# Block attention and expert layers on one core: the last pair's softmax sums on TensorE, weight copies and squares moved between engines, slot 0's second layer moved ahead of slot 1

## The chip, the cores and the metric

The kernel runs on one core of a Trainium2 chip. The metric is the time of one execution on the device, in microseconds (us); lower is better. Of the kernel before, three runs were timed and one more execution was profiled.

## What is computed

```python
scores = scale * np.matmul(q, k.transpose(0, 1, 3, 2))      # q, k, v: 8 x 8 x 576 x 64
scores = np.where(block_i >= block_j, scores, -1e9)         # blocks of 64 positions
attn = exp(scores - max);  attn = attn / sum(attn)
x = (attn @ v), heads side by side                          # 4608 tokens x 512
logits = normalised x @ normalised expert_emb.T / tau       # 8 experts
expert = argmax(logits);  gate = softmax(logits)[expert]
out[token] = gate * (relu(x @ w1[expert]) @ w2[expert])     # w1 512 x 1024, w2 1024 x 512
```

Attention is block-causal. Each token then goes through one of eight experts, the one with the largest logit.

## The kernel before

**Attention.** The 64 heads are worked on in 32 pairs (n = 0 to 31), a pair being two heads of one batch. `scores` makes the scores transposed, keys on the partitions, in five key tiles t of 128 keys (the last has 64); ScalarE takes the exponentials into `pT` (L378, L385). `add` (L359) has GpSimd add the tiles t = 1 to 4 into `pS`, so that `pS` and tile 0 hold, per query, what has to be summed over 128 partitions. One pair later `values` multiplies the probabilities with V into the PSUM tile `psb` (L398), ScalarE copies the result to `oe` (L404), and TensorE sums with matmuls whose stationary side is the constant `ones` with 32 columns: four column groups g, one for each 128 queries (L413, L416). Beside them come the router's logits from `enT` and `oe`. `su` (L418) takes the sums out of PSUM. `finish` turns `su` and `oe` by TensorE (L428, L430), divides on VectorE (L435 to L445, which read `psb`), stores rows and, in the last batch, takes squares on ScalarE (`squares`, L464). The pool `ps_b` has one buffer, so the values of a pair wait until `finish` of the pair before has read it.

**The order.** In the loop over pairs a string of letters (`PLANS`) writes the order out by hand: s is a step of `scores`, v of `values` of the pair before, f of `finish` of that pair, r of the router. Each engine and the queues of SyncE (SP) and GpSimd (POOL) execute in program order.

**Between attention and experts.** Weights arrive as f32 in `raw0` (w1) and `raw1` (w2), in four chunks of 128 x 1024 (c = 0 to 3). Each chunk is split into a high part `ring_h` (a rounding copy, `split_hi`, L731) and a low part `ring_l` (raw minus high, `split_lo`, L736, on VectorE); a product is three matmuls, high·high, low·high and high·low (`mm3`, L931). A ring tile has two halves. Two "early" slots a and b of 128 tokens (`ex0`, `ex1`) hold tokens of expert 0 from the first seven batches; their rows are gathered by GpSimd (L584). While the last pair is finished and the last batch is routed, TensorE works on a and b: `xt` turns their rows (L918), ScalarE and VectorE split these into high and low (L921, L922), `l1` and `l2` are the two layers. `chain()` is the routing of the last batch, step by step between the pieces of `l1` and `l2`: `finish` of pair 31, `route`, `counts`, `slot_tokens`, and the gathers of the first slots (`fetch`, L909). `second(c)` makes the high and low part of chunk c of expert 0's w2; `again` the same for the other ring; `next_weights` those of expert 1.

**Slots.** Then slots g of 128 tokens each follow: `layer1` (24 matmuls), `xt` of the next slot, the turn of h, and the second layer of the slot before. For slot 1 the turn is done by TensorE (`mixed`, `ht`); for later slots by VectorE (L977).

The steps that the change touches, as they stand before:

```python
for c in range(NPC):                       # L1061
    split_hi(0, c, 0, eng=nc.gpsimd if c == 2 else nc.scalar)
    split_lo(0, c, 0)
    if c < 2:
        drain(pv, 4)                       # values of pair 31
    if c == 1:
        drain(pv)                          # sums of pair 31
        for u, g in enumerate(ea):
            xt(g, pts[u], hx if u else None)
```

Of the kernel before, what the change touches and what calls it, by code (L numbers as in the profile page):

```python
# [8 lines left out]
F32 = mybir.dt.float32  # L9
# [25 lines left out]
def kernel(  # L35
# [12 lines left out]
    nc = tc.nc  # L48
# [312 lines left out]
    def scores(n, pTs):  # L361

        i = n % NBUF
        for hh, (pT, ps) in enumerate(pTs):

            def mm(o, t, c0, c1):
                ts = slice(t * P, (t + 1) * P)
                nc.tensor.matmul(o, ka[i][:, hh, ts], qb[i][:, hh, c0:c1], start=True, stop=False)  # L368
                nc.tensor.matmul(o, kx[i][0:KX, hh, ts], qx[i][0:KX, hh, c0:c1], start=False, stop=True)  # L369

            for t, c0, c1 in ((0, 0, S // 2), (0, S // 2, S), (1, P, S), (2, 2 * P, S)):
                if n == 0 and hh and c0 == 0:
# [12 lines left out]
            nc.scalar.activation(pT[:, off[3]:NPT], st[:, 0:256], AF.Exp, scale=scale)  # L385
            add(ps, 3, pT)
            add(ps, 4, pT)
            yield

    def values(n, pTs):  # L390

        a = vo[n % NV]
        ob = ps_b.tile([P, 1024], F32, name="psb")
        for t in range(NJ):
# [10 lines left out]
        yield  # L405
        for w in range(3):
            for g in range(NG):
                if w == 2:
                    a, m = enT[:, n % NP], o[:, g * P:(g + 1) * P]
                else:  # L410
                    pT, ps = pTs[w]
                    a, m = ones[:, w], ps[:, (g - 1) * P:g * P] if g else pT[:, 0:P]
                nc.tensor.matmul(ob[32 * g:32 * g + 32, 0:P], a, m, start=(w == 0), stop=(w == 2))  # L413
        for g, (a, m) in enumerate(((enT[:, n % NP], o[:, S - 64:S]),) + tuple(
                (ones[:, w % 2], pTs[w % 2][1][:, S - P - 64:S - P]) for w in range(3))):
            nc.tensor.matmul(ob[32 * g:32 * g + 32, P:LW], a, m, start=True, stop=True)  # L416
        yield
        nc.scalar.copy(su[n % 2][:, 0:LW], ob[:, 0:LW])  # L418
        yield

    def finish(n, xrow, rin, lgh, ssp):
# [29 lines left out]
        if n >= NPAIR - NP:  # L451
            yield "squares"
            for j in range(NJ):
                squares(xrow[:, j, hp * P:(hp + 1) * P], ssp[:, j, hp:hp + 1])
            yield

    def store(b, xrow, c0, c1):
# [11 lines left out]
    def route(b, xrow, lgh, ssp):  # L469
# [532 lines left out]
    def chain():  # L1002
# [15 lines left out]
        tw = two()  # L1018
        yield next(tw)
        next(rg)  # L1020
        for _ in range(5):
# [28 lines left out]
    hx = [mx.tile([P, NF // 2, P], F32R, name=nm) for nm in ("hh1", "hl1")]  # L1050
    psum_t.close()
    ps_e = pool(psum_t, "ps_e", 1, space=PSUM)
    pts = [ps_e.tile([P, 512], F32, name=f"pe{u}") for u in range(2)]
    ea = []
    for u in range(EARLY):
# [3 lines left out]
        slots[g]["w", 0] = half_of(0, 0)  # L1059
        slots[g]["w", 1] = half_of(0, 1)  # L1060
    for c in range(NPC):  # L1061
        split_hi(0, c, 0, eng=nc.gpsimd if c == 2 else nc.scalar)
        split_lo(0, c, 0)
        if c < 2:
            drain(pv, 4)
        if c == 1:
            drain(pv)
            for u, g in enumerate(ea):
                xt(g, pts[u], hx if u else None)
    load_raw(0, 1)  # L1070
# [52 lines left out]
    def second(c):  # L1123
        split_hi(1, c, 1, to=0)
        split_lo(1, c, 1, to=0)
# [6 lines left out]
    second(0)  # L1132
    drain(last_f)
    drain(ch_sq[0])
# [25 lines left out]
    next_weights(0, 0, (0, 1, 2))  # L1160
    l2(b, range(6, 7))
    for f in range(0, DF, 512):
        l1(0, range(NC1), f)
    xt(1, pts[1])
    l2(b, range(7, 8))
    fetch(AHEAD)
# [21 lines left out]
    def mixed(g):  # L1188

        pts = turn_pe(g)  # L1190
        out = take("py")
        mm3(g - 1, 1, out, slots[g - 1]["hT"], DM, NF, 0, range(4))
# [6 lines left out]
    def back(g):  # L1199
# [8 lines left out]
        if g == 1:  # L1208
            next_weights(0, 1, range(NPC))
            next_high(1, 0, range(NPC))  # L1210
# [38 lines left out]
    TURNED, FLAGS_AT = (1,), 1  # L1249
    pt0 = turn_pe(0)  # L1250
    ht(0, (0, 4), pt0, ("turn",))
    ht(0, (0, 4), pt0, ("split",))
    next_weights(0, 0, (3,))
    flags(1)
# [54 lines left out]
```

## Time and profile before

| | us |
|---|---|
| median of three runs | 867.73 (865.12 to 867.75) |
| profiled execution, its own time | 863.76 |
| its span | 862.0 |
| TensorE busy in the span | 829.6 |

The profiled execution is one more run, 3.97 us under the median; its span is the time from its first instruction to its last, 1.76 us less than its time. Attention fills the span up to about 402 us, the two early slots and the routing of the last batch reach to about 441 us, and the slots fill the rest at 11.4 us each. In rows of the timeline, the two numbers ahead of the engine are start and length in us; what stands in brackets is how long the engine was idle before, and who released it.

### The profile page before, as it was taken

To read this page: it belongs to the slowest core of one execution; us is meant where nothing else is said; L and a number is where in the kernel's file an instruction comes from. 1 tells how busy PE (TensorE), PEld (TensorE's weight loads), DVE (VectorE), ACT (ScalarE), POOL (GpSimd) and SP (SyncE) were. 2 spreads that over 40 slices of the span, in tenths; PEclk is the share of its full clock that TensorE was granted. 3 is DMA by queue.
4 is the path that set the end of the run, shared out by engine and by line. 5 is a ranking of instruction groups with operands and counts; after the bars stand their busy time and mean duration, and the time that the engine had idled before them with its cause. 6 is when DMAs were issued, how large, how long until landed. Compare 5 with 4: busy or idle time off the path is not lost. (4 is left out here: it accounts for less than half of the span.)

```text
span 862.0 us, 20599 instructions
## 1 busy us (share of the span) xinstructions
PE 829.6 (96%) x5609; PEld 663.7 (77%) x5609; DVE 658.3 (76%) x1539; ACT 479.0 (56%) x1027; POOL 447.6 (52%) x509
## 2 busy tenths in 40 slices
PE   5999999999999999997999999899999999999997
PEld 4777777777778887776778888688878888888885
DVE  7678878787878888764867887677887777778871
ACT  4566868676767868775565446454443233442232
POOL 5355575756567575676134647876472111572101
PEclk9999999999999999999999999999999999999999
DMA  7777777879677887837175525555252111012111
GB/s 153 168 164 162 181 190 180 210 172 219 153 195 161 211 176 158 205 111 245 55 253 176 172 96 174 190 177 185 86 180 90 52 51 51 28 49 72 39 35 48
DMA packets 155176, 122.31 MB, mean 142 GB/s; under 512 B 122217, under 2 KB 123513, under 8 KB 155020
## 3 DMA queue, kind: packets, MB, share of 16 engines
q1 hardware_dynamic: 147372, 100.14, 44.9%
q0 software_dynamic: 7648, 20.44, 7.4%
q8 instruction: 55, 0.90, 0.4%
q14 instruction: 101, 0.83, 0.3%
HBM read 72.71 MB, written 19.71 MB: 107 GB/s over the span
## 5 line engine op out<-in xcount | busy, mean ns | idle before, releaser
L977 DVE STREAM_TRANSPOSE pt<-h 32x256 f32<-32x256 f32 x528 | 240.7, 456 | 18.0
L339 DVE TENSOR_REDUCE nmx<-psm 128x1 f32<-128x320 f32 x315 | 135.5, 454 | 54.8 <-PE psm L338 50.0
L378 ACT ACTIVATE pT<-pss 128x448 f32<-128x448 f32 (+1 forms) x254 | 109.0, 450 | 83.2 <-PE pss L369 80.3
L991 POOL DMA_INDIRECT out_dram<-y,outi x36 | 35.8, 994 | 192.1 <-ACTq L885 138.1
L736 POOL TENSOR_TENSOR ring_l<-raw,ring_h 128x1024 f32 (+1 forms) x49 | 116.3, 2401 | 30.8 <-ACT ring_h L731 23.3
L359 POOL TENSOR_TENSOR pS<-pS,pT 128x320 f32<-128x320 f32 (+2 forms) x192 | 115.1, 600 | 27.2 <-ACT pT L378 10.4
L368 PE MATMUL pss<-qb,ka 128*128 128x448 f32 (+1 forms) x382 | 118.4, 322 | 0.0
L359 POOL TENSOR_TENSOR pS<-pT 128x448 f32<-128x448 f32 x64 | 73.1, 1142 | 78.5 <-ACT pT L378 77.9
L931 PE MATMUL py<-ring_h,hh 128*128 (+1 forms) x280 | 112.5, 402 | 1.1 <-ACT hh L983 0.6
L931 PE MATMUL py<-ring_h,hl 128*128 (+1 forms) x280 | 111.6, 398 | 0.8 <-DVE hl L985 0.8
L369 PE MATMUL pss<-qx,kx 70*128 70x448 f32 (+1 forms) x382 | 109.8, 310 | 1.3 <-DMA qx<-nmT 1.1
L931 PE MATMUL ph<-ring_l,xh 128*128 x280 | 109.2, 390 | 1.6 <-POOLq L897 0.9
L931 PE MATMUL ph<-ring_h,xh 128*128 x280 | 109.2, 390 | 0.7 <-ACT ring_h L731 0.7
L931 PE MATMUL py<-ring_l,hh 128*128 (+1 forms) x280 | 109.3, 390 | 0.0
L931 PE MATMUL ph<-ring_h,xl 128*128 x280 | 109.1, 390 | 0.0
L338 PE MATMUL psm<-kd,qd 128*128 128x320 f32 x315 | 106.6, 361 | 1.8 <-ACT kd L318 1.8
L398 PE MATMUL psb<-pT,vo 128*64 128x64 f32 (+4 forms) x768 | 99.2, 399 | 6.0 <-DVE lgh L445 5.5
L949 ACT ACTIVATE h<-ph 128x512 f32<-128x512 f32 x70 | 42.0, 600 | 90.0 <-DVE pt L977 78.9
L985 DVE TENSOR_TENSOR hl<-pt,hh 128x512 fp32r<-128x512 f32 x66 | 42.5, 687 | 61.2 <-ACT hh L983 59.0
L990 ACT ACTIVATE y<-py,xg 128x512 f32<-128x512 f32 x35 | 24.1, 688 | 110.6 <-PE py L931 110.6
L398 PEld LDWEIGHTS psb<-pT,vo 128*64 128x64 f32 x768 | 49.9, 138 | 44.3 <-issue 30.7
L731 ACT CAST ring_h<-raw 128x1024 f32 (+1 forms) x67 | 66.2, 1048 | 27.7 <-SPq L904 11.9
(260 smaller groups left out, 1622.5 us busy)
## 6 DMA issues: line engine op xcount, KB each, us to landing
raw<-in_moe_w_dram SPq DMA_DIRECT2D x64, 512.0 KB
ka<-kd SPq DMA_DIRECT2D x128, 144.0 KB
qn<-in_q_dram SPq DMA_DIRECT2D x64, 144.0 KB
kn<-in_k_dram SPq DMA_DIRECT2D x64, 144.0 KB
qx<-qb SPq DMA_DIRECT2D x32, 288.0 KB
vo<-in_v_dram SPq DMA_DIRECT2D x64, 128.0 KB
xbuf<-xrow SPq DMA_DIRECT2D x7, 1040.0 KB
qx<-nmT SPq DMA_DIRECT2D x64, 2.2 KB
```

The lines of the kernel that those rows point to most:

```text
L338: nc.tensor.matmul(mx[:, 0:e - a], qd[d][:, j, :, :], kd[d][:, a:e], start=True, stop=True)
L339: nc.vector.tensor_reduce(m[:, j + u:j + u + 1], mx[:, 0:e - a], axis=AX.X, op=ALU.max, negate=True)
L359: nc.gpsimd.tensor_tensor(o, pT[0:r, P:S] if t == 1 else o, pT[0:r, off[t]:off[t] + w], op=ALU.add)
L368: nc.tensor.matmul(o, ka[i][:, hh, ts], qb[i][:, hh, c0:c1], start=True, stop=False)
L369: nc.tensor.matmul(o, kx[i][0:KX, hh, ts], qx[i][0:KX, hh, c0:c1], start=False, stop=True)
L378: nc.scalar.activation(pT[:, o:o + c1 - c0], st[:, 0:c1 - c0], AF.Exp, scale=scale)
L398: nc.tensor.matmul(ob[hh * D:(hh + 1) * D, c0:c1], a[:, t, hh, :], pTs[hh][0][:, o:o + c1 - c0], start=(t == 0), stop=(c0 == 448 or t == N ...
L731: return (nc.scalar.copy if eng is nc.scalar else eng.tensor_copy)(piece(ring_h, to, c, half), raw[i][:, c * CW:(c + 1) * CW])
L736: return eng.tensor_tensor(piece(ring_l, to, c, half), raw[i][:, c * CW:(c + 1) * CW], piece(ring_h, to, c, half).bitcast(F32), op=ALU.sub ...
L931: m = nc.tensor.matmul(out, ac, w, start=(c == 0 and w is wh and a is sh), stop=(c == nk - 1 and a is sl_))
L977: nc.vector.transpose(pt[32 * j:32 * j + 32, :, 32 * i:32 * i + 32], h[32 * i:32 * i + 32, :, j, :])
L985: nc.vector.tensor_tensor(sets["hl"][u], pt[:, 4 * u:4 * u + 4], sets["hh"][u].bitcast(F32), op=ALU.subtract)
```

## The change

Five edits, all of them between the last pair of attention and slot 2:

1. Pair 31 does without GpSimd's adds. Its sums are made by TensorE from `pT` directly: for each head and key tile t, one matmul for each group g ≥ t (20 of 128 columns in place of 8) and 11 of 64 columns in place of 3. Its values go to the tile `pst`, its sums to `psb`.
2. The high parts of w1 of expert 0 are made in the order c = 2, 0, 1, 3, chunks 2 and 3 on GpSimd, 0 and 1 on ScalarE; all four low parts on VectorE come before `xt` of the early slots. The four high parts of expert 0's w2 follow on GpSimd; they were ScalarE's in `second`.
3. The squares of pair 30 are taken after the early slots' rows are split, in place of ahead of the weight copies.
4. In `chain()` three steps of `counts` come ahead of the sum of squares, and one more step of the routing is put between the power (on GpSimd) and the addition that reads it.
5. The turn of slot 0's h goes into the PSUM tiles of the early slots; `next_weights` of expert 1's w2 and slot 0's second layer come ahead of slot 1's first layer. `mixed(1)` is left with the turn and split of slot 1's h.

The diff, cut to this:

```diff
@@ scores
-                if t > 0:
+                if t > 0 and n < NPAIR - 1:
                     add(ps, t, pT)
...
-            add(ps, 3, pT)
-            add(ps, 4, pT)
+            for t in range(3, NJ if n < NPAIR - 1 else 3):
+                add(ps, t, pT)
@@ values
-        ob = ps_b.tile([P, 1024], F32, name="psb")
+        ob = ps_b.tile([P, 1024], F32, name="psb") if n < NPAIR - 1 else ps_t.tile([P, 1024], F32, name="pst")
...
+        sb = ob if n < NPAIR - 1 else ps_b.tile([P, 1024], F32, name="psb")
...
+            for w in range(2):
+                for t in range(NG):
+                    for g in range(t, NG):
+                        c = off[t] + (g - t) * P
+                        nc.tensor.matmul(sb[32 * g:32 * g + 32, 0:P], ones[:, w], pTs[w][0][:, c:c + P],
+                                         start=(w == 0 and t == 0), stop=False)
+            tail = [[(w % 2, pTs[w % 2][0][:, off[t] + S - 64 - t * P:off[t] + S - t * P], t == t0, t == NJ - 1)
+                     for t in range(t0, NJ)] for w, t0 in ((0, 0), (1, 0), (0, NJ - 1))]
+            yield
+        for g in range(NG):
+            nc.tensor.matmul(sb[32 * g:32 * g + 32, 0:P], enT[:, n % NP], o[:, g * P:(g + 1) * P],
+                             start=False, stop=True)
...
@@ finish
-            for j in range(NJ):
-                squares(xrow[:, j, hp * P:(hp + 1) * P], ssp[:, j, hp:hp + 1])
+            if n == NPAIR - 2:
+                late.append(lambda: parts_squares(hp, xrow, ssp))
+            else:
+                parts_squares(hp, xrow, ssp)
@@ route
         nc.gpsimd.tensor_tensor(ss, ss, half, op=ALU.pow)
+        if b == B - 1:
+            yield
         eng.tensor_scalar(ss, ss, 1.0e-6, None, op0=ALU.add)
@@ chain
         yield next(tw)
+        yield next(tw)
+        yield next(tw)
         next(rg)
@@ between attention and experts
-    for c in range(NPC):
-        split_hi(0, c, 0, eng=nc.gpsimd if c == 2 else nc.scalar)
-        split_lo(0, c, 0)
...
+    for c in (2, 0, 1, 3):
+        split_hi(0, c, 0, eng=nc.gpsimd if c > 1 else nc.scalar)
+        split_lo(0, c, 0)
+    for c in range(NPC):
+        split_hi(1, c, 1, to=0, eng=nc.gpsimd)
+    drain(pv)
...
+    for u, g in enumerate(ea):
+        xt(g, pts[u], hx if u else None)
+    drain(last_f)
+    late.pop()()
@@ second
-        split_hi(1, c, 1, to=0)
         split_lo(1, c, 1, to=0)
@@ slot 0
-    xt(1, pts[1])
-    l2(b, range(7, 8))
+    ht(0, (0,), pts, ("turn",))
+    ht(0, (0,), pts, ("split",))
+    xt(1, ps_m.tile([P, 512], F32, name="psm"))
+    ht(0, (4,), pts, ("turn",))
+    l2(b, (7,))
+    ht(0, (4,), pts, ("split",))
+    next_weights(0, 0, (3,))
+    next_weights(0, 1, range(NPC))
+    py = ps_b.tile([P, 1024], F32, name="psb")[:, 0:DM]
+    mm3(0, 1, py, slots[0]["hT"], DM, NF, 0)
+    give(0, py, slots[0]["xg"][:, DM:DM + 1], outi[:, 0:1])
```

How the instructions move is shown at three places. The first is TensorE from the last values of pair 31 to the first layer of early slot a. Before:

```order
L398 MATMUL psb<-pT,vo_166 64x192 x2
L398 MATMUL psb<-pT,vo_166 64x64 x2
L413 MATMUL psb<-pT,ones 32x128
L413 MATMUL psb<-pS,ones 32x128 x3
L413 MATMUL psb<-pT,ones 32x128
L413 MATMUL psb<-pS,ones 32x128 x3
L413 MATMUL psb<-oe_198,enT 32x128 x4
L416 MATMUL psb<-oe_198,enT 32x64
L416 MATMUL psb<-pS,ones 32x64 x3
L918 MATMUL pe_6370<-ident,ex_206 128x128 x4
```

The same place in the changed kernel:

```order
L398 MATMUL pst<-pT,vo_166 64x192 x2
L398 MATMUL pst<-pT,vo_166 64x64 x2
L420 MATMUL psb<-pT,ones 32x128 x20
L426 MATMUL psb<-oe_198,enT 32x128 x4
L428 MATMUL psb<-oe_198,enT 32x64
L433 MATMUL psb<-pT,ones 32x64 x11
L945 MATMUL pe_6416<-ident,ex_206 128x128 x4
```

No matmul reads `pS` any more, the sums have another PSUM tile than the values, and there are 20 + 11 sums in place of 8 + 3.

The second place is VectorE after `finish` of pair 30. `ring_l` with `raw_126` are low parts of w1, `xl` and `hl` the low parts of the early slots' rows. Before:

```order
L445 TENSOR_TENSOR lgh<-psb,rin 128x16
L736 TENSOR_TENSOR ring_l_6351<-raw_126,ring_h_6350 128x1024 x2
L922 TENSOR_TENSOR xl_6363<-pe_6370,xh_6362 128x512
L922 TENSOR_TENSOR hl_6365<-pe_6371,hh_6364 128x512
L736 TENSOR_TENSOR ring_l_6351<-raw_126,ring_h_6350 128x1024 x2
L435 TENSOR_SCALAR rin<-psb 128x4x2
```

And in the changed kernel:

```order
L462 TENSOR_TENSOR lgh<-psb,rin 128x16
L763 TENSOR_TENSOR ring_l_6333<-raw_126,ring_h_6332 128x1024 x4
L949 TENSOR_TENSOR xl_6345<-pe_6416,xh_6344 128x512
L949 TENSOR_TENSOR hl_6347<-pe_6417,hh_6346 128x512
L452 TENSOR_SCALAR rin<-psb 128x4x2
```

Four low parts stand ahead of `xl`, where two stood.

The third place is ScalarE from the last weight copies of the early stage to slot 1 (`hh` high parts of h, `y` an output tile, `tb` flags of a slot). Before:

```order
L990 ACTIVATE y_6435<-pss,ex_207 128x512
L965 CAST hh_6433<-pt_6802 128x512
L965 CAST hh_6364<-pt_6802 128x512
L731 CAST ring_h_6350<-raw_126 128x1024
L865 TENSOR_LOAD tb_6442
```

And in the changed kernel:

```order
L992 CAST hh_6346<-pe_6417 128x512
L758 CAST ring_h_6332<-raw_126 128x1024
L758 CAST ring_h_6636<-raw_6334 128x1024 x4
L1017 ACTIVATE y_6453<-psb,xg_6455 128x512
L892 TENSOR_LOAD tb_6459
```

Four copies of expert 1's w2 and the output of slot 0 now stand ahead of slot 1's flags and activations; before, the copies came behind them.

## Rows read from the trace of the kernel before

**Rows 1.** The page's first part: busy time, share of the span, instructions, by engine.

```profile
PE 829.6 (96%) x5609; PEld 663.7 (77%) x5609; DVE 658.3 (76%) x1539; ACT 479.0 (56%) x1027; POOL 447.6 (52%) x509
```

**Rows 2.** Stretches: window, length, busy PE, PEld, DVE, ACT, POOL (instructions), granted clock, DMA share, GB/s.

```profile
383.20:394.20 11.00, 9.00 (x87) 6.33 (x88) 2.28 (x9) 7.50 (x26) 8.92 (x17) 1.00 0.09 22
398.00:402.30 4.30, 1.70 (x32) 1.05 (x32) 3.14 (x2) 0.61 (x2) 4.07 (x5) 1.00 1.02 337
404.00:406.30 2.30, 2.30 (x6) 1.77 (x7) 2.14 (x3) 1.53 (x2) 0.00 (x0) 0.55 1.06 417
441.00:450.00 9.00, 7.57 (x38) 5.58 (x37) 3.97 (x5) 3.69 (x7) 1.98 (x2) 1.00 0.81 306
```

**Rows 3.** Timeline of TensorE (PE), from pair 31's values to early slot a.

```profile
394.22 2.92 PE L398 MATMUL psb<-pT,vo 128*64 128x64 f32 x24 [1.07 <-DVE lgh L445]
398.67 0.30 PE L413 MATMUL psb<-pT,ones 128*32 128x128 f32 x1 [1.52 <-ACT oe L404]
...
402.31 1.68 PE L918 MATMUL pe<-ident,ex 128*128 128x128 f32 x8
403.81 0.79 PE L931 MATMUL pss<-ring_h,xh 128*128 128x512 f32 x1
...
407.24 0.39 PE L931 MATMUL pss<-ring_l,xh 128*128 128x512 f32 x1
407.47 0.39 PE L931 MATMUL pss<-ring_h,xl 128*128 128x512 f32 x1
```

**Rows 4.** Waits, 380 to 475 us: us in total, times, longest.

```profile
PE psb L413 <- POOL pS L359: 1.9, 2, 1.1
DVE ss L535 <- POOL ss L534: 1.3, 1, 1.3
DVE ss L533 <- ACT xs L464: 0.8, 1, 0.8
PE pss L931 <- DVE ring_l L736: 0.7, 2, 0.4
```

**Rows 5.** Timeline of ScalarE (ACT), 396 to 399 us.

```profile
396.08 1.99 ACT L731 CAST ring_h<-raw 128x1024 fp32r<-128x1024 f32 x2
397.98 0.63 ACT L404 COPY oe<-psb 128x576 f32<-128x576 f32 x1
```

**Rows 6.** Timeline of TensorE, slot 1 and the turn to slot 2.

```profile
444.96 0.51 PE L931 MATMUL ph<-ring_h,xh 128*128 x1 [0.68 <-ACT ring_h L731]
446.23 0.50 PE L931 MATMUL ph<-ring_l,xh 128*128 x1 [0.76 <-DVE ring_l L736]
...
449.56 0.60 PE L918 MATMUL px<-ident,xg 128*128 128x128 f32 x4
449.91 0.47 PE L931 MATMUL py<-ring_h,hh 128*128 128x512 f32 x1
```

**Rows 7.** Timeline of TensorE, the sums of pair 30.

```profile
389.86 0.30 PE L413 MATMUL psb<-pT,ones 128*32 128x128 f32 x1
...
390.32 0.40 PE L413 MATMUL psb<-oe,enT 128*32 128x128 f32 x8
```

**Rows 8.** Timeline of GpSimd (POOL), around the last adds.

```profile
393.03 0.98 POOL L584 DMA_INDIRECT ex<-xbuf,ei  x1 [0.30 <-issue]
...
401.93 1.03 POOL L731 CAST ring_h<-raw 128x1024 fp32r<-128x1024 f32 x1
```

**Rows 9.** Line 736 on VectorE (DVE): duration in ns, least, median, most; first and last start.

```profile
L736 DVE TENSOR_TENSOR ring_l<-raw,ring_h x19: 1210/1222/2679, 397.2 to 455.3; 128x1024 fp32r<-128x1024 f32 x19
```

**Rows 10.** Timeline of VectorE, two low parts and the first low row part.

```profile
397.16 3.98 DVE L736 TENSOR_TENSOR ring_l<-raw,ring_h 128x1024 fp32r<-128x1024 f32 x2 [3.09 <-ACT ring_h L731]
403.79 0.69 DVE L922 TENSOR_TENSOR xl<-pe,xh 128x512 fp32r<-128x512 f32 x1 [2.65 <-ACT xh L921]
```

**Rows 11.** Timeline of ScalarE, slot 1's second activation and expert 1's w2.

```profile
449.82 0.60 ACT L949 ACTIVATE h<-ph 128x512 f32<-128x512 f32 x1 [2.17 <-PE ph L931]
...
450.78 3.90 ACT L731 CAST ring_h<-raw 128x1024 fp32r<-128x1024 f32 x4
```

More of the change, by code (lines that the diff above doesn't have):

```diff
@@ L405, in values @@
         yield
[L406 to L410, printed above, removed]
-                    pT, ps = pTs[w]
[L412 to L416, printed above, removed]
+        sb = ob if n < NPAIR - 1 else ps_b.tile([P, 1024], F32, name="psb")
@@ new lines, in values @@
+        if n < NPAIR - 1:
+            for w in range(2):
+                for g in range(NG):
+                    pT, ps = pTs[w]
+                    nc.tensor.matmul(sb[32 * g:32 * g + 32, 0:P], ones[:, w],
+                                     ps[:, (g - 1) * P:g * P] if g else pT[:, 0:P], start=(w == 0), stop=False)
+            tail = [(w % 2, pTs[w % 2][1][:, S - P - 64:S - P], True, True) for w in range(3)]
+            tail = [[u] for u in tail]
+        else:
+            for w in range(2):
+                for t in range(NG):
[6 more added lines that the diff above has]
+            yield
@@ new lines, in values @@
+        for g in range(NG):
+            nc.tensor.matmul(sb[32 * g:32 * g + 32, 0:P], enT[:, n % NP], o[:, g * P:(g + 1) * P],
+                             start=False, stop=True)
+        nc.tensor.matmul(sb[0:32, P:LW], enT[:, n % NP], o[:, S - 64:S], start=True, stop=True)
+        for u in range(max(len(t) for t in tail)):
+            for g, t in enumerate(tail, 1):
+                if u < len(t):
+                    w, m, first, done = t[u]
+                    nc.tensor.matmul(sb[32 * g:32 * g + 32, P:LW], ones[:, w], m, start=first, stop=done)
@@ L417, in values @@
         yield
-        nc.scalar.copy(su[n % 2][:, 0:LW], ob[:, 0:LW])
+        nc.scalar.copy(su[n % 2][:, 0:LW], sb[:, 0:LW])
         yield
@@ L452, in finish, with parts_squares @@
             yield "squares"
-            for j in range(NJ):
-                squares(xrow[:, j, hp * P:(hp + 1) * P], ssp[:, j, hp:hp + 1])
+            if n == NPAIR - 2:
+                late.append(lambda: parts_squares(hp, xrow, ssp))
+            else:
+                parts_squares(hp, xrow, ssp)
             yield
+    late = []
+    def parts_squares(hp, xrow, ssp):
+        for j in range(NJ):
+            squares(xrow[:, j, hp * P:(hp + 1) * P], ssp[:, j, hp:hp + 1])
     def store(b, xrow, c0, c1):
@@ L1060 @@
         slots[g]["w", 1] = half_of(0, 1)
+    for c in (2, 0, 1, 3):
+        split_hi(0, c, 0, eng=nc.gpsimd if c > 1 else nc.scalar)
+        split_lo(0, c, 0)
     for c in range(NPC):
-        split_hi(0, c, 0, eng=nc.gpsimd if c == 2 else nc.scalar)
-        split_lo(0, c, 0)
[L1064 to L1069, printed above, removed]
+        split_hi(1, c, 1, to=0, eng=nc.gpsimd)
+    drain(pv)
+    psum_t.close()
+    ps_e = pool(psum_t, "ps_e", 1, space=PSUM)
+    pts = [ps_e.tile([P, 512], F32, name=f"pe{u}") for u in range(2)]
+    for u, g in enumerate(ea):
+        xt(g, pts[u], hx if u else None)
+    drain(last_f)
+    late.pop()()
     load_raw(0, 1)
@@ L1132 @@
     second(0)
-    drain(last_f)
     drain(ch_sq[0])
@@ L1190, in mixed @@
         pts = turn_pe(g)
+        if g == 1:
+            ht(g, (0, 4), pts, ("turn",))
+            ht(g, (0, 4), pts, ("split",))
+            return
         out = take("py")
@@ L1249 @@
     TURNED, FLAGS_AT = (1,), 1
[L1250 to L1253, printed above, removed]
     flags(1)
```

6 lines of the change are left out of this document (1 added, 5 removed).

## The prediction

> **What bounds the kernel now.** I read the engines' totals first: TensorE is busy 829.6 us of a span of 862.0 [rows 1], so only its idle time, and time at a lower clock, can be won. The table by stretches then tells where both lie [rows 2]: from 398.00 to 402.30 TensorE is busy 1.70 of 4.30 us, behind it the granted clock is 0.55 (1.2 GHz for most of the stretch), and from 441.00 to 450.00 it is busy 7.57 of 9.00. The other engines matter only where TensorE waits for them, so the timeline of TensorE is read next, wait by wait, with the queues that end each. Pair 31's values wait 1.07 us for VectorE to read the tile `psb`; the sums wait 1.52 us for ScalarE's copy `oe` [rows 3] and 1.9 us for GpSimd's adds [rows 4]. In slot 1's first layer TensorE waits 0.68 us for the high and 0.76 us for the low part of expert 1's last w1 chunk [rows 6]. Whatever is won on TensorE in these places reaches the end, because the slots behind them keep it busy.
>
> **Values and sums.** With a tile of their own the values start 1.07 us earlier, at 394.22 - 1.07 = 393.15, and end 2.92 us later at 396.07 [rows 3]. Nothing waits for `pS` now. The sums cost more TensorE time: for pair 30, eight matmuls of 128 columns took 390.32 - 389.86 = 0.46 us [rows 7], so four column groups that run abreast take 0.23. The twenty of the change come per head as 4, 3, 2 and 1 groups, eight rounds: 8 x 0.23 = 1.84 us. Four for the logits take 0.23, and the 64-column tail, at half the columns, five rounds of 0.115, 0.58. Together 2.65 us: they end at 398.72, where before they ended at 402.31. The copy `oe` is needed at 396.07 + 1.84 = 397.91. It ended at 397.98 + 0.63 = 398.61 when the squares stood ahead of the two weight copies [rows 5]; with the squares moved behind the rows' split it runs beside the sums. That edit is costed at nothing; if the cover failed, it would cost 398.61 - 397.91 = 0.7 us.
>
> **From the sums to early slot a.** Its first matmul came 403.81 - 402.31 = 1.50 us behind the first transpose [rows 3], so now at 400.2 at the latest. Its third needs `xl`, and four low parts stand ahead of `xl` in VectorE's queue. They begin when GpSimd has copied chunk 2: the gather ends at 393.03 + 0.98 = 394.01, the copy takes 1.03 [rows 8], so 395.05. Four at the median of 1.22 us [rows 9] end at 399.95. Beside GpSimd's adds two took 3.98, 1.99 each [rows 10]. GpSimd's copies beside VectorE's low parts are not in this trace; the bounds are no slowing at all, and one low part slowed by 0.77 us (GpSimd's next copy covers about one; the four of w2 must first wait for their load). With `xl` at 0.69 us [rows 10] that gives 400.6 to 401.4; I take 401.0, between two rows of the same instruction. Ten matmuls are left, 407.47 - 407.24 = 0.23 us apart [rows 3]: they end at 403.3, where they ended at 407.47 + 0.23 = 407.70. **Term: 4.4 us** (4.0 to 4.8). This leaves the clock at 2.4 GHz, the first rival's subject. The w2 copies moved to GpSimd hide behind the routing, in which GpSimd has nothing else to do; the waits of TensorE did not end on them.
>
> **The routing.** VectorE stood still 0.8 us for the last squares and 1.3 us for GpSimd's power, with the slot counts queued behind both, and TensorE then waited 0.7 us in two places for low parts behind these steps [rows 4]. The steps now stand ahead. The bounds are 0 (the new order lets VectorE wait elsewhere: `gx` on ScalarE comes later) and 2.1, the whole stall; TensorE can win no more than it waited, so I take **0.5 us**.
>
> **Slots 0 and 1.** Twenty-four matmuls of 0.23, 5.5 us, are put ahead of slot 1's first layer. The high and low part that it waited for are done by then, so 0.68 + 0.76 = 1.44 us go. What is late next: the turn of slot 1's h follows the transposes of slot 2 directly. The second half of the turn needs the activation that ran from 449.82 to 450.42 [rows 11]; four transposes take 449.91 - 449.56 = 0.35 us [rows 6], so TensorE would arrive at 449.56 + 2 x 0.35 = 450.26 and wait about 0.2. Slot 2's first layer then needs its rows split, about 0.6 us on ScalarE and 0.69 on VectorE behind that activation, at 451.0 and 451.7, where TensorE is at 450.8 and, for the third matmul, 451.2: another 0.4 to 0.5. The turn of slot 0 waits for its activation likewise, 0.2. **Term: 1.44 - 0.85 = 0.6 us** (0 to 1.44). SP's loads of the next weights are freed earlier by the early copies; the gather of slot 3's rows on POOL now queues behind slot 0's output, some 7 us later, but is needed a whole slot after that.
>
> **The sum.** 4.4 + 0.5 + 0.6 = 5.5 us. From the profiled execution's own 863.76 that makes 858.3. That execution lay 3.97 us under the median of 867.73; on the scale of the median the forecast is 867.73 - 5.5 = **862.2 us**. A difference under 0.3%, 2.6 us, can't be told from no change with this kernel.
>
> **Rivals.**
>
> *The clock falls all the same.* Between 396.07 and 401.0 TensorE runs narrow sums and eight transposes and waits about 1.5 us. Before, 1.2 GHz followed a stretch in which it was busy 1.70 of 4.30. Against it: it kept 1.00 through 9.00 of 11.00 and through 7.57 of 9.00 busy [rows 2], nearer to what I expect. Price: eight transposes took 1.5 us to the first matmul where two times 0.35 would do, 0.8 us; the twelve took 407.70 - 403.81 = 3.89 where 2.76 would do, 1.1, part of it the wait for `xl`. I take 1.6: 863.8 us. Chance 0.25.
>
> *VectorE and GpSimd hold each other up, and early slot a starts late: slower.* If each of the four low parts takes 2.68 us, the longest [rows 9], `xl` is ready at 395.05 + 10.72 + 0.69 = 406.5; TensorE has idled 5 us and gets 1.2 GHz, where six matmuls took 2.30 us, 0.38 each [rows 2]. Ten end at 410.3, 2.6 us late; the other terms give back 1.1, so 869.2 us. It decides from 2.3 us for a low part on. For it: 1.99 in place of 1.22 beside the adds. Against: two copies of 1.03 can't cover four low parts. By the Trainium skill, GPSIMD Engine Reference, Specifications, GpSimd shares its SBUF interfaces with VectorE and contends with VectorE instructions that have two SBUF inputs; the low parts have two, and the 3.98 us agree with it. Chance 0.05.
>
> *Slot 1 waits behind ScalarE's new copies.* The four copies of expert 1's w2 took 3.90 us from 450.78 without a wait [rows 11]; nothing in that row says that their load had landed earlier. If it lands only then, slot 1's activation comes after 450.78 + 3.90, the output's 0.69 and some 2 us of flags, at about 457.4, while its first layer ends near 449.56 - 1.44 + 5.5 = 453.6: 3.8 us lost, 866.0 us. Chance 0.10.
>
> *The sums don't run abreast.* With three, two and one group in order, twenty might go one by one: 20 x 0.23 - 1.84 = 2.8 us more, and 0.7 in the tail. Early slot a then starts at about 403.7 with `xl` ready and ends at 406.5: 1.2 in place of 4.4, in all 2.3, or 865.4 us. Against it: the same column groups ran abreast in pair 30 [rows 7]. Chance 0.08.
>
> **How the numbers follow.** The forecast has 0.52. It and the clock rival lie over 2.6 us faster, 0.77; a good half of the others' cases is within 2.6 us, and slower by more needs low parts slower than any row has. So faster 0.78, same 0.18, slower 0.04. The low end of the range takes the better bounds, 4.8 + 1.5 + 1.4 = 7.7, and two more us, since single runs lie between 863.76 and 867.75: 858. The high end, 866, takes in the clock, sums one by one and the late load; about 2 in 10 stay out.
>
> **What would show it.** Right: no wait of the last sums for an add; the early slots' transposes near 398.7 and the third matmul of slot a by 401.4, granted clock 1.00 from 398 on; no idle time in slot 1's first layer, and under 1 us between the turn of slot 1's h and slot 2's layer. Wrong: low parts near 2 us or more, a clock of 0.5 behind 399, a wait on ScalarE's activation of slot 1 over 1 us, or idle time of TensorE at slot 0's row transposes for the gather.

## The result, and the profile after

The changed kernel took **859.42 us** (median of 5, 859.12 to 861.27) against 867.75 beside it (865.12 to 868.45): ratio 0.9914, 95% interval 0.9887 to 0.994, 8.3 us less. The forecast was 862.2 us, faster, range 858 to 866. Direction and range held; the gain was forecast too small. The profiled execution took 859.12 us, its span 857.3. First its page, the answer to [rows 1], with the row of TensorE's granted clock in 40 slices:

```profile
PE 828.1 (97%) x5649; PEld 663.3 (77%) x5649; DVE 656.9 (77%) x1539; ACT 473.2 (55%) x1022; POOL 446.2 (52%) x506
...
PEclk8699999999999999999999999999999999999999
```

TensorE is busy 1.5 us less in a span 4.7 us shorter: most of the gain is idle time. The clock's two low digits at the start are some 20 us at 1.2 GHz, which the first profile of before did not have. The second profile of the changed kernel did not have them either, so they don't come from the change; what they cost can't be told, since the last scores come at 393.53 to 394.63 us in the three profiles that have them and at 392.87 to 395.27 in the eleven others. So positions are compared from one landmark (a row that every trace has) to the next, not from the start. The timeline of TensorE, from the last scores to the last slot, for [rows 3] and [rows 6]:

```profile
393.93 0.28 PE L369 MATMUL pss<-qx,kx 70*128 70x64 f32 x1
394.13 2.92 PE L398 MATMUL pst<-pT,vo 128*64 128x64 f32 x24
396.99 1.63 PE L420 MATMUL psb<-pT,ones 128*32 128x128 f32 x37
...
399.35 1.09 PE L945 MATMUL pe<-ident,ex 128*128 128x128 f32 x8
400.74 0.50 PE L958 MATMUL pss<-ring_h,xh 128*128 128x512 f32 x1 [0.29 <-ACT xh L948]
...
402.22 0.50 PE L958 MATMUL pss<-ring_h,xl 128*128 128x512 f32 x1 [0.74 <-DVE xl L949]
...
404.63 0.38 PE L445 MATMUL psb<-ident,su 128*128 128x128 f32 x2
...
428.97 0.51 PE L958 MATMUL psm<-ring_h,xh 128*128 128x512 f32 x1
...
447.96 0.60 PE L945 MATMUL px<-ident,xg 128*128 128x128 f32 x4
448.40 1.13 PE L988 MATMUL pt<-ident,h 128*128 128x128 f32 x8
450.11 0.50 PE L958 MATMUL ph<-ring_h,xh 128*128 x1 [0.58 <-ACTq L912]
...
455.73 0.60 PE L945 MATMUL px<-ident,xg 128*128 128x128 f32 x4
...
827.38 0.60 PE L945 MATMUL px<-ident,xg 128*128 128x128 f32 x4
```

Neither the values nor the sums wait now. The two waits of [rows 6] are gone, and one of 0.58 us stands behind the turn of slot 1's h. These rows cut the kernel into four stretches: **front** (last scores, 393.93, to `su`'s transposes, 404.63, which follow early slot a's first twelve matmuls), **routing** (to slot 0's first layer, 428.97), **slots 0, 1** (to the transposes of slot 3's rows, 455.73) and **slots 3 on** (to those of the last slot, 827.38). The same rows, read in every profile:

| kernel | front | routing | slots 0, 1 | slots 3 on | profiled | median | ratio (95%) |
|---|---|---|---|---|---|---|---|
| before | 14.83 | 26.28 | 27.84 | 370.16 | 863.76 | 867.75 | |
| before_again | 14.87 | 26.26 | 27.81 | 373.39 | 867.31 | | |
| before_third | 15.61 | 26.25 | 27.88 | 373.81 | 868.40 | | |
| **after** | 10.70 | 24.34 | 26.76 | 371.65 | 859.12 | 859.42 | 0.9914 (0.9887 to 0.994) |
| after_again | 10.75 | 24.35 | 26.76 | 373.13 | 860.26 | 860.01 | 0.9914 (0.9887 to 0.9942) |
| u1_adds | 21.46 | 24.88 | 26.73 | 372.75 | 872.09 | 872.80 | 1.0058 (1.0036 to 1.0079) |
| u2_w2highs | 10.73 | 24.50 | 26.77 | 372.99 | 860.73 | 861.34 | 0.9926 (0.9902 to 0.995) |
| u3_squares | 11.23 | 24.43 | 26.74 | 372.69 | 861.10 | 862.69 | 0.9938 (0.9915 to 0.9961) |
| u4_chain | 10.72 | 25.79 | 26.72 | 374.04 | 863.08 | 862.70 | 0.9931 (0.9907 to 0.9955) |
| u5_slot | 10.77 | 24.37 | 27.82 | 373.11 | 862.70 | 862.64 | 0.9941 (0.9921 to 0.996) |
| a1_sums | 11.21 | 26.28 | 27.82 | 373.71 | 863.91 | 865.17 | 0.9954 (0.9934 to 0.9974) |
| i1_xl | 9.96 | 24.40 | 26.75 | 374.68 | 861.70 | 860.36 | 0.9903 (0.9882 to 0.9923) |
| i2_casts | 9.95 | 24.34 | 26.77 | 373.67 | 861.57 | 861.57 | 0.991 (0.9879 to 0.9941) |
| i3_back | 9.95 | 24.39 | 26.76 | 380.82 | 865.96 | 865.99 | 0.9971 (0.9953 to 0.9988) |

The first three stretches repeat within 0.2 us from execution to execution of a kernel (before's front apart, 0.8), far better than the times, which spread over 5 us and more. Against the first profile of before the change wins 4.13 + 1.94 + 1.08 = **7.15 us** in them. The medians move by up to 2 us more than the stretches (`u4_chain` and `u5_slot` 2.7 and 2.6 us above `after_again` for 1.4 and 1.1); their intervals are about 2 us to either side, so verdicts on small parts go by the stretches. The times that the theories below name for `u1_adds`, `u3_squares`, `u4_chain` and `u5_slot` were exceeded by 1 to 2 us; where that lies was not found.

The windows that answer to [rows 2]:

```profile
399.40:404.60 5.20, 4.16 (x22) 3.04 (x21) 3.36 (x4) 3.30 (x13) 0.94 (x1) 1.00 1.04 322
441.00:450.00 9.00, 8.53 (x44) 6.92 (x42) 4.64 (x5) 4.21 (x7) 2.95 (x2) 1.00 0.99 303
```

The clock is 1.00 through early slot a, where it was 0.55 from 404.0 to 406.3 before.

VectorE (with the least, median and longest duration of its four low parts, in ns), GpSimd and ScalarE in the front, for [rows 5], [rows 8] to [rows 10]; one fence each:

```profile
396.13 5.43 DVE L763 TENSOR_TENSOR ring_l<-raw,ring_h 128x1024 fp32r<-128x1024 f32 x4 [1.00 <-POOL ring_h L758]
401.49 0.68 DVE L949 TENSOR_TENSOR xl<-pe,xh 128x512 fp32r<-128x512 f32 x1
```

```profile
L763 DVE TENSOR_TENSOR ring_l<-raw,ring_h x4: 1211/1212/2029, 396.1 to 400.4; 128x1024 fp32r<-128x1024 f32 x4
```

```profile
395.05 2.02 POOL L758 CAST ring_h<-raw 128x1024 fp32r<-128x1024 f32 x2
```

```profile
394.63 1.99 ACT L758 CAST ring_h<-raw 128x1024 fp32r<-128x1024 f32 x2
397.10 0.64 ACT L404 COPY oe<-pst 128x576 f32<-128x576 f32 x1 [0.48 <-PE pst L398]
```

Of the four low parts the first took 2.03 us, 0.81 more than the median of [rows 9]; it began at 396.13, while GpSimd's second copy ran, which ended at 397.07. The other three took 1.21 each, with GpSimd idle. It is so in all nine profiles that have the new order and the sums on TensorE. `xl` follows them, and is what TensorE waits 0.74 us for.

### The profile page after: what moved, and what is told of

It reads as the page before. It is cut to its first block, busy times and chain, and to the rows that moved or that the text cites. A ratio compares the mean times of both kernels' runs of the same rounds, so it can differ in the third digit from the quotient of the medians.

```text
span 857.3 us, 20666 instructions
## 1 busy us (share of the span) xinstructions
PE 828.1 (97%) x5649; PEld 663.3 (77%) x5649; DVE 656.9 (77%) x1539; ACT 473.2 (55%) x1022; POOL 446.2 (52%) x506
## 5 line engine op out<-in xcount | busy, mean ns | idle before, releaser
L359 POOL TENSOR_TENSOR pS<-pS,pT 128x320 f32<-128x320 f32 x186 | 109.9, 591 | 26.7 <-ACT pT L378 10.4
L359 POOL TENSOR_TENSOR pS<-pT 128x448 f32<-128x448 f32 x62 | 70.8, 1141 | 80.1 <-ACT pT L378 79.6
L958 PE MATMUL py<-ring_h,hh 128*128 x272 | 109.2, 401 | 2.0 <-ACT hh L1010 2.0
L958 PE MATMUL py<-ring_h,hl 128*128 x272 | 108.5, 399 | 1.7 <-DVE hl L1012 1.7
L958 PE MATMUL py<-ring_l,hh 128*128 x272 | 106.3, 391 | 0.0
L398 PE MATMUL psb<-pT,vo 128*64 128x64 f32 (+1 forms) x744 | 97.1, 402 | 4.9 <-DVE lgh L462 4.8
L368 PEld LDWEIGHTS pss<-qb,ka 128*128 128x128 f32 x382 | 73.9, 193 | 6.7 <-ACT pT L378 1.2
```

The lines of the kernel that those rows point to most:

```text
L359: nc.gpsimd.tensor_tensor(o, pT[0:r, P:S] if t == 1 else o, pT[0:r, off[t]:off[t] + w], op=ALU.add)
L398: nc.tensor.matmul(ob[hh * D:(hh + 1) * D, c0:c1], a[:, t, hh, :], pTs[hh][0][:, o:o + c1 - c0], start=(t == 0), stop=(c0 == 448 or t == N ...
L958: m = nc.tensor.matmul(out, ac, w, start=(c == 0 and w is wh and a is sh), stop=(c == nk - 1 and a is sl_))
```

## The experiments

Names in `u` undo one part of the changed kernel, `a1` makes one part alone on the kernel before, names in `i` try to better it. No edit was made for `after_again`, `before_again` and `before_third`.

**after_again.** 

> The changed kernel unaltered, to see what differs between two executions of one program. From the pair's scores to slot 2's first layer the changed trace gained 7.3 us (front 4.1, routing 1.9, slots 1.3), and from there to the end it lost 1.35 us against before, in single waits of 0.24 to 0.48 us for the low half of a slot's h near 468, 526 and 588 us. Theory of chance: in those slots two of ScalarE's four weight copies landed behind a late load and ahead of the activation; when a load lands varies from execution to execution, so here the waits stand in other slots or are fewer, and the difference to before in the timed runs is again nearer 7 us than the 4.7 us of the two profiles. Rival, the shift: the change moves the slots against the loads, so the same three waits come back in the same three slots. The first 100 us may again show 1.2 GHz for some 20 us or not (the other changed runs have mean clocks of 0.982 to 0.999). Time 858.5 to 861.5 us by both.

The first three stretches came back within 0.05 us. The waits in the slots came back too: 0.28 us at 468.22 where it was 0.24, and the slots at 524.5 and 587.8 lost 0.86 and 0.98 us against 11.42 a slot, where they had lost 0.84 and 0.78. So they are not the chance of one execution. But only the wait near 468 is the change's: in the profiles of before that slot lost 0.12 to 0.16 us, with the change 0.44 and 0.48, and with edit 5 undone (`u5_slot`) 0.14 again. The slots of the other two waits lost 0.61 and 0.84 us in `before_again`, and 0.79 and 1.44 in `before_third`; the first profile of before, which lost nothing there, is the exception, and the shift does not hold for them. The two rows of `before_again` on TensorE:

```profile
532.40 0.50 PE L931 MATMUL py<-ring_h,hl 128*128 x1 [0.39 <-DVE hl L985]
...
596.28 0.51 PE L931 MATMUL py<-ring_h,hl 128*128 x1 [0.48 <-DVE hl L985]
```

What differed between the two profiles of the changed kernel was the double change of experts near 552 us (two experts' weights are made one right after the other there), by 1.3 us over two slots. The windows of the first profile, then of this one:

```profile
549.00:553.00 4.00, 1.48 (x7) 0.72 (x6) 0.37 (x1) 3.85 (x7) 2.75 (x3) 1.00 0.18 48
553.00:557.00 4.00, 3.63 (x16) 3.02 (x17) 3.80 (x9) 2.43 (x5) 4.00 (x3) 1.00 0.30 87
```

```profile
549.00:553.00 4.00, 1.27 (x6) 0.92 (x6) 0.15 (x1) 3.63 (x6) 3.07 (x3) 0.90 0.21 54
553.00:557.00 4.00, 4.00 (x13) 2.77 (x12) 3.83 (x8) 2.43 (x5) 4.00 (x3) 0.68 0.24 63
```

TensorE idles about as long in both, 2.5 to 2.7 us of four; only in the second does the clock fall to 1.2 GHz (0.90 and 0.68 are means with 2.4 GHz).

**before_again, before_third.** 

> The kernel before, unaltered, profiled once more. Its first profile (863.76 us, mean clock 0.997) lies under nearly all its timed executions (863.3 to 871.55, mean clocks mostly 0.980 to 0.997), so it may not show what the median of 868 holds. Theory: most executions of before hold a second stretch at 1.2 GHz behind a place where TensorE idles (the sums at 396 to 402, slot 1's first layer at 440 to 447, or the double change of experts at 549 to 559), which this one execution was spared at some of them; then this profile, if its time is 866 us or more, shows a granted clock near 0.5 for 5 to 12 us in all there, and the rest of the difference between the medians (8.3 to 8.6 us) and the profiles (4.7 us) is clock. Rival: it is idle time, waits for late loads of weights behind 460 us, at a clock of 1.00.

> The kernel before once more. The two profiles of it lost 4.6 and 8.0 us against 11.42 us a slot from slot 3 to the end; the second had 1.2 GHz from about 559.5 to 563 us, the first had not. Theory: this one is like the second (its time 866 us or more, the granted clock falling behind the double change of experts near 560 us). Rival: the first is the common case: under 865 us, clock 1.00 there.

Both show what the first profile of before had been spared. TensorE in `before_again`, waits and then windows:

```profile
556.66 0.66 PE L918 MATMUL px<-ident,xg 128*128 128x128 f32 x4 [1.49 <-DMA xg<-xbuf,rowi]
558.49 0.50 PE L931 MATMUL py<-ring_h,hh 128*128 x1 [1.16 <-ACT hh L983]
```

```profile
555.00:559.00 4.00, 1.34 (x7) 0.72 (x6) 0.05 (x1) 3.53 (x6) 2.87 (x3) 1.00 0.25 60
559.00:563.00 4.00, 3.52 (x9) 2.64 (x9) 3.83 (x8) 2.42 (x5) 4.00 (x3) 0.62 0.29 74
```

From slot 3 on they take 373.39 and 373.81 us where the first profile took 370.16: 3.2 and 3.7 us more, as clock and as waits that are longer or that the first did not have, so theory and rival each hold a part. This accounts for much of why the profiles of the two kernels lay only 4.7 us apart where the medians lie 8.3 apart. The third has a longer front too, 15.61: its mean clock was 0.79 from 398 to 402 us already, where the other two had 1.00.

**u1_adds**, sums and values undone:

```diff
-                if t > 0 and n < NPAIR - 1:
+                if t > 0:
...
-            for t in range(3, NJ if n < NPAIR - 1 else 3):
+            for t in range(3, NJ):
...
-        ob = ps_b.tile([P, 1024], F32, name="psb") if n < NPAIR - 1 else ps_t.tile([P, 1024], F32, name="pst")
+        ob = ps_b.tile([P, 1024], F32, name="psb")
...
-        sb = ob if n < NPAIR - 1 else ps_b.tile([P, 1024], F32, name="psb")
-        if n < NPAIR - 1:
+        sb = ob
+        if n < NPAIR:
```

> The last pair's sums go back to the added probabilities, and its values back into the shared tile; all else stays changed. By the theory of the trace (GpSimd's copy of chunk 2 is the head of the low parts' queue): GpSimd's adds end near 402, its copy of chunk 2 follows at about 403, four low parts at 1.2 to 2 us and the split of the rows put the third matmul of early slot a at 409 to 412, so TensorE idles for 6 us or more, perhaps at 1.2 GHz behind it; the twelve end at 411 to 415 in place of 404.6 and the time is 866 to 871 us, no better than before. Rival: the sums themselves were the worth of the change (TensorE waited 1.9 us for the adds and 1.07 for the tile), the low parts overlap, and the loss is 3 to 4 us: 862.5 to 863.5 us.

872.80 us, slower than before by 0.58% (0.36 to 0.79). VectorE, GpSimd, then the windows:

```profile
402.24 7.96 DVE L763 TENSOR_TENSOR ring_l<-raw,ring_h 128x1024 fp32r<-128x1024 f32 x4 [7.21 <-POOL ring_h L758]
410.12 0.68 DVE L949 TENSOR_TENSOR xl<-pe,xh 128x512 fp32r<-128x512 f32 x1
```

```profile
401.18 9.92 POOL L758 CAST ring_h<-raw 128x1024 fp32r<-128x1024 f32 x6
```

```profile
406.00:410.00 4.00, 0.80 (x1) 0.29 (x1) 4.00 (x3) 0.00 (x0) 4.00 (x3) 0.51 0.54 161
410.00:415.00 5.00, 4.15 (x10) 3.28 (x11) 1.40 (x3) 0.00 (x0) 1.10 (x1) 0.50 0.79 294
```

With the adds back in GpSimd's queue its copy of chunk 2 ends at 402.2, the four low parts follow, and the clock falls: the front takes 21.46 us. The theory of the trace holds; the parts of the change don't add up, the new order of the high copies *needs* the sums on TensorE. The low parts take 2.03 to 2.05 us each here, all four beside copies on GpSimd, of which four take 2.03 in place of 1.03; in the changed kernel only the first low part meets a copy. That GpSimd and VectorE contend for SBUF where a VectorE instruction has two SBUF inputs, as the Trainium skill says (GPSIMD Engine Reference, Specifications), agrees with these rows.

**a1_sums**, the same part alone on the kernel before. Its diff is the first pieces of the change's (scores and values); the early slots' PSUM tiles are opened behind the last values, which use the pool that they replace.

> The kernel before with the first part of the change alone: the last pair's sums from the probabilities on TensorE, its values in a tile of their own; highs, squares, routing and slots as before. From the scores' last matmul to the end of early slot a's first twelve took 14.83 and 14.87 us in the two profiles of before, 10.70 and 10.75 with the whole change, and 21.46 with this part alone undone. Theory: this part is the lever of the front, and the shared highs and late squares are worth 0.5 to 1.1 us more; the stretch here is 11.2 to 11.9 us, the clock stays at 1.00 behind the sums, the routing takes its old 26.3 and the slots their old 27.8, and the time is 864 to 866 us. Rival: without the shared highs the copy oe and the low parts stay late, TensorE idles as long as before and falls to 1.2 GHz again: 13 us or more, 867 us.

Front 11.21, routing and slots as before, 865.17 us: the theory. This part alone is 3.6 of the front's 4.1 us.

**u3_squares**

```diff
-            if n == NPAIR - 2:
+            if n == -1:
...
-    late.pop()()
```

> The squares of pair 30 go back to their old place, ahead of ScalarE's two weight copies; all else stays changed. Theory (the prediction's price if the cover failed): the copy oe ends 0.7 us later than the sums want it, TensorE waits for it, and with the high parts of chunks 0 and 1 later too the third matmul of early slot a is 0.5 to 1.5 us later: 860.2 to 861.5 us. Rival: the third matmul waits for the low parts anyway, which start with GpSimd's chunk, so the sums may end later without any effect, and the time is within 0.3 us of the change's.

Front 11.23, the theory at its lower end. TensorE:

```profile
399.89 0.43 PE L426 MATMUL psb<-oe,enT 128*32 128x128 f32 x8 [0.79 <-ACT oe L404]
```

The wait for `oe` that the prediction priced at 0.7 us appears, 0.79; the front loses 0.5, since the wait for `xl` goes in return. Front 11.23 is also that of `a1_sums`, which has neither the late squares nor the shared highs: behind early squares, the shared highs are worth nothing in the front.

**u2_w2highs**

```diff
-    for c in range(NPC):
-        split_hi(1, c, 1, to=0, eng=nc.gpsimd)
...
     def second(c):
+        split_hi(1, c, 1, to=0)
         split_lo(1, c, 1, to=0)
```

> The four high copies of expert 1's w2 go back from GpSimd to ScalarE, next to their low parts; all else stays changed. With the routing's order undone the stretch from early slot a's twelve matmuls to slot 0 took 25.79 us, not the 26.28 of before, so 0.5 us is left over. Theory: these copies are what is left, since ScalarE made them in the routing ahead of the activations: the stretch is 24.8 us in place of 24.34 and the time 860.0 to 860.5 us. Rival, the predicted nothing: ScalarE idles there 2.7 to 4 us at a time, so the stretch stays within 0.1 of 24.34 and the time within 1 us of the change's 859.4 to 860.0.

The copies are those of expert 0's w2, as edit 2 has it, not expert 1's. Routing 24.50, 0.16 us more: between the two, nearer to the rival's 0.1 than to the theory's 0.5. The median, 861.34, is over what either named, but can't be told from the change's.

**u4_chain**

```diff
-        if b == B - 1:
-            yield
...
         yield next(tw)
-        yield next(tw)
-        yield next(tw)
```

> The routing's steps go back to their old order behind the counts; all else stays changed. The stretch from the end of early slot a's first twelve matmuls to slot 0's first layer took 26.28 us before and 24.34 with the change. Theory of the trace: the new order is what won 1.9 us there, because TensorE waited for low parts queued behind VectorE's two stops; undone, the stretch is 25.8 to 26.3 us, TensorE waits 0.7 us and more for low parts again and the time is 860.8 to 861.5 us. Rival, the predicted size: 0.5 us, 859.9 us, the rest of the 1.9 coming from the w2 copies on GpSimd, which ScalarE no longer has to make there.

Routing 25.79: 1.45 of the 1.94 us are this order. The waits that return, on TensorE:

```profile
418.43 0.50 PE L956 MATMUL pss<-ring_l,hh 128*128 128x512 f32 x1 [0.33 <-DVE ring_l L761]
...
422.22 0.50 PE L956 MATMUL pss<-ring_l,hh 128*128 128x512 f32 x1 [0.41 <-DVE ring_l L761]
422.55 0.39 PE L956 MATMUL pss<-ring_h,hl 128*128 128x512 f32 x1
```

Read as idle time they are 0.74 us. Set against the same steps of the changed kernel, counted from `su`'s transposes, the transposes of h behind the first come 0.69 us later and those behind the second another 0.76. A wait costs more than the idle time shown: matmuls start 0.23 us apart but are recorded as 0.39 long, so the first 0.16 of a wait lies under the one before; and the first behind a wait takes about 0.34 to the next, 0.11 more. That is 0.27 of the 0.36 and 0.35 us; the rest stays open.

In before a third such wait, 0.26 for `rowto`, was worth 0.43. It is gone in `u2`, `u3` and `u4` alike, and is back in `a1_sums`. The traces show two edits that remove it, each without the other. In before a copy of w2 stood ahead of pair 31's squares on ScalarE, VectorE waited 0.8 us for them ahead of its sum `ss`, and `rowto` stood behind that sum. With w2's copies on GpSimd (`u4`) the sum no longer waits; with the counts ahead of it (`u2`) `rowto` no longer stands behind it. The sum in `u4`, then in `a1_sums`, which has neither edit:

```profile
412.60 0.17 DVE L558 TENSOR_REDUCE ss<-ssp 128x5 f32<-128x20 f32 x1
```

```profile
412.88 0.18 DVE L550 TENSOR_REDUCE ss<-ssp 128x5 f32<-128x20 f32 x1 [0.80 <-ACT xs L481]
```

Counted from `su`'s transposes `rowto` starts at 11.72 us in `u4` and at 12.19 in `a1_sums`. Undoing one of two such edits shows nothing of what they share. Both undone, with all else changed, was not run.

**u5_slot.** The last piece of the change's diff undone (`slot 0`), with the turn of slot 0's h and its second layer back at their old places.

> Slot 0's second layer goes back behind slot 1's first layer; all else stays changed. Theory of the trace: the waits of 0.68 and 0.76 us for the high and low part of expert 1's last w1 chunk return, 1.3 us in all up to slot 2's first layer, and the time is 860.7 us. Rival, the weight chain: with the front 4 us earlier the loads of expert 1's weights are not earlier, so the waits grow by as much as TensorE has gained on them, 2 us or more, and the time is 862 us or more. Rival, the predicted size: 0.6 us, 860.0 us.

Slots 0, 1 take 27.82, 1.06 us more. The waits are those of [rows 6], to 0.01 us:

```profile
440.76 0.49 PE L958 MATMUL ph<-ring_h,xh 128*128 x1 [0.67 <-ACT ring_h L758]
442.01 0.50 PE L958 MATMUL ph<-ring_l,xh 128*128 x1 [0.76 <-DVE ring_l L763]
```

TensorE's gain ahead of them does not make them longer, so the copies behind which they stand move with it; the rival falls, though the time, 862.64 us, is what it named. The three steps from 439.70 to 442.35 take 2.65 us where 0.68 would do: 1.97 lost, 1.43 shown.

**i1_xl**

```diff
-        split_lo(0, c, 0)
+        if c < 3:
+            split_lo(0, c, 0)
...
+    split_lo(0, 3, 0)
```

> An attempt to better both: the low part of the fourth chunk moves behind the split of the early slots' rows on VectorE, so that three low parts, not four, stand ahead of xl. The third matmul of early slot a waited 0.74 to 0.80 us for xl; one low part takes 1.36 us. Theory: that wait goes, and with it the refill behind it, 0.7 to 1.0 us in all; the fourth chunk's low part is then wanted by the eleventh matmul some 2.3 us behind the first, and is done by about 402, in time. Time 858.4 to 859.0 us. Rival: the wait moves to that low part (it follows xl and hl, two splits of 0.69 us), 0.3 us or less is won.

The wait for `xl` is gone and the front is 9.96, 0.74 us better than the change's, and the same within 0.01 us in all three kernels that hold this edit. The time, 860.36 us, is over the theory's 859.0 and can't be told from the change's; the profiled execution had 1.2 GHz from about 552 to 559 us.

**i2_casts**, on `i1_xl`:

```diff
-        layer1(g, None if "hT" in slots[g - 1] else lambda: split_h(g - 1))
+        def between():
+            if "hT" not in slots[g - 1]:
+                split_h(g - 1)
+            next_high(g - 1, 1, (0, 1))
+            next_low(g - 1, 1, (0, 1))
+        layer1(g, between)
...
-        next_high(g, 1, (0, 1))
...
-        next_low(g, 1, (0, 1))
```

> The kernel i1_xl with one more move, in the slots: ScalarE's first two high copies of the next expert's w2 (and GpSimd's low parts of them) go from the end of a slot to behind the next slot's first activation and the copies hh. In every profile but the first of before, TensorE waited 1.7 to 1.9 us at the double change of experts near 552 us (1.16 in before's second) for hh, which stood on ScalarE behind two copies whose load landed late, and in most of them the clock fell to 1.2 GHz for 2 to 8 us behind it. Theory: this wait and the waits of 0.24 to 0.48 us in the slots near 468 and 588 go, the clock stays at 1.00, and with the copies 2 us later in the slot ahead of it TensorE waits up to 2 us for the last low part near 544 (0.33 us now): the slots from slot 3 to the end lose 4 to 6 us against 11.42 us each in place of 6.3 to 9.4, and the time is 857 to 859 us. Rival: GpSimd's eight low parts in a row (18.9 us) bound that place, the wait near 544 grows by 2.5 us or more and brings the slow clock with it: no better than 860 us.

The wait near 552 us went and the clock stayed at 1.00 there. That agrees with what was taken to make the wait: `hh` stood behind copies whose load was late. For the clock it is one profile, and `u1_adds` kept 1.00 there without this edit. But the slots at 491, 598, 645 and 772 us each lost 1.1 us, which the changed kernel doesn't show, and the wait near 546 grew to 1.19. The theory's 857 to 859 us was missed: 861.57, no better.

**i3_back**, the two copies joined to the other two in `back`:

```diff
-        next_high(g - 1, 1, (2, 3))
-        next_low(g - 1, 1, (2, 3))
+        next_high(g - 1, 1, range(NPC))
+        next_low(g - 1, 1, range(NPC))
```

> As i2_casts, but the two copies stand behind the slot's second activation and the split of the next rows, together with the other two of w2, so that no branch stands between activations. In i2_casts the wait of 1.8 us near 552 us and the slow clock behind it were gone, but slots at 491, 598, 645 and 772 us lost 1.1 us each, where ScalarE's second activation came 0.4 to 0.7 us late behind the new branches. Theory: those four losses go too, the slots from slot 3 on lose 4 to 5 us against 11.42 each, most of it near 546 us where the eight low parts now start 3 us later than with the change, and the time is 856 to 858.5 us. Rival: the eight low parts bound the double change, the wait there grows to 3 us or more and takes back what was won, at 859 us or more.

A miss: 865.99 us. TensorE at the double change, and the window behind it:

```profile
547.41 0.79 PE L958 MATMUL ph<-ring_l,xh 128*128 x1 [3.61 <-POOLq L924]
...
568.85 0.50 PE L958 MATMUL py<-ring_l,hh 128*128 x1 [1.45 <-POOLq L924]
```

```profile
547.50:552.00 4.50, 4.50 (x11) 3.53 (x12) 0.00 (x0) 0.00 (x0) 1.99 (x2) 0.50 0.84 262
```

GpSimd's eight low parts (18.8 us) start at 528.57 here and bound the place, as the rival had it. Besides the 3.61 us, five waits for low parts of w2 take 7.1 us together. No version clearly beat the changed kernel.

## Why the prediction was right, and where it was off

**Values and sums: right.** The wait for `psb` is gone (values 0.20 us behind the start of the last scores), and the sums run abreast: from 396.99 to the transposes at 399.35, 2.36 us for the 2.65 worked out. The copy `oe` waited for nothing but the values (397.10), and `u3_squares` shows what the cover was worth: 0.79 us of wait for the 0.7 named, 0.5 us of the front.

**To early slot a: right, 4.1 for 4.4.** On before's positions (its last scores 1.06 us earlier) the third matmul came at 401.16, forecast 401.0, and the twelve ended at 403.57, forecast 403.3. The upper bound's mechanism came true, one low part slowed by 0.81 us for the 0.77 named; `xl` was ready at 401.11 and not 401.4, because low parts start 1.13 us apart and not 1.22. The clock stayed at 2.4 GHz: the first rival didn't come. That this was near is seen in `u1_adds`: the second rival's mechanism, low parts at 2 us and a late `xl`, is what the new order does without the sums, and it ends slower than before.

**The routing: wrong in size, 1.94 for 0.5.** The step that failed is "TensorE can win no more than it waited, so I take 0.5". The waits that before shows are these:

```profile
420.14 0.90 PE L794 MATMUL psm<-rowto,xg 96*128 96x43 f32 x6 [0.26 <-DVE rowto L788]
...
421.67 0.50 PE L931 MATMUL pss<-ring_l,hh 128*128 128x512 f32 x1 [0.33 <-DVE ring_l L736]
...
425.47 0.50 PE L931 MATMUL pss<-ring_l,hh 128*128 128x512 f32 x1 [0.41 <-DVE ring_l L736]
```

They make 1.0 us, and of these it counted 0.7. Set against the changed kernel, step by step from `su`'s transposes, they cost 0.43 + 0.73 + 0.78 = 1.94, the whole gain. That the whole stall of VectorE, 2.1 us, lay near it is no proof that it was the right measure. The w2 copies on GpSimd, costed at nothing, are worth 0.16 us beside the new order (`u2_w2highs`); with the old order they are what takes the `rowto` wait away (`u4_chain`).

**Slots 0 and 1: 1.08 for 0.6, the same error.** The two waits were worth 1.97, not 1.44. New waits take back about 0.9, as forecast (0.85); 0.58 of it shows, at 450.11. Behind this stretch another 0.3 us goes back, in the wait near 468 that comes with this edit. ScalarE's copies ahead of slot 1 show no wait for their load, so that rival fell:

```profile
438.11 4.85 ACT L758 CAST ring_h<-raw 128x1024 fp32r<-128x1024 f32 x5
442.86 0.68 ACT L1017 ACTIVATE y<-psb,xg 128x512 f32<-128x512 f32 x1
445.79 0.60 ACT L976 ACTIVATE h<-ph 128x512 f32<-128x512 f32 x1 [2.25 <-PE ph L958]
```

They end 2.8 us before slot 1's first activation (third row), which waits for TensorE, as it should.

**The sum: 7.15 for 5.5.** 1.44 of the missing 1.65 us is the routing, 0.48 the slots, less 0.27 at the front. That the range held is in part luck: the better bounds of the three terms add up to 7.7 us, with 1.5 for the routing, which gave 1.94; alone they end at 860.0, above the 859.42 measured, and the two more us for the spread of single runs took it in. The timed difference of 8.3 (8.1 in the second comparison) is about 1 us more. Part of it may be that before's front is longer in some executions (15.61 in one of three profiles). Whether the slots too lose less on average with the change stays open: three profiles of before and two of the change, 370.16 to 373.81 and 371.65 and 373.13, don't tell.

**The scale: a choice that proved right.** The sum was set on the median, not on the one profile. That profile was the exception: it was spared the 1.2 GHz near 560 us.

## What to carry to other kernels

A wait of TensorE costs more than the idle time the profile shows beside it, here 0.17 to 0.40 us more for each: price short waits by when the next landmark comes, not by the bracket. Cut a kernel at landmarks and compare stretches; that told 0.1 us apart where whole executions spread over 5. And take parts of a change that share an engine's queue as one: with the sums moved, the shared high copies and late squares gained 0.5 us in the front (10.70 against 11.21 in `a1_sums`); without, they cost 6.6 (21.46 in `u1_adds` against before's 14.83). And where two edits cure the same wait, undo both: undone singly, each seems worth nothing.

## What was not expected of the hardware

The granted clock fell to 1.2 GHz for 3 to 7 us between 545 and 570 us in 10 of the 14 profiles, and not in the first of before, the first of the change, `u1_adds` and `i2_casts`: the same program with nearly the same idle time did either. The Trainium skill (TensorE: Matmul & The Clock Gate, Part 1) says that how many matmuls at a kernel's start run at the low clock varies from run to run of one kernel; in the middle of a kernel the two profiles of the changed kernel show such a difference, 1.00 against 0.68 from 553 to 557 us. Three profiles (the first of the change, `u5_slot`, `a1_sums`) also had 1.2 GHz for some 20 us of the first 50; the other eleven had none there.

A low part on VectorE took 2.03 us beside a copy on GpSimd and 1.21 alone. Where the two engines kept meeting, in `u1_adds`, GpSimd's copy took 2.03 too, for 1.03 alone.
